# A one-core attention, expert and feed-forward kernel: the first pair's queries loaded and prepared ahead of its keys, and the early weights loaded into rooms that are free

## The chip, the cores and the metric

One core of a Trainium2 chip runs the whole program in one launch. The metric is the device time in microseconds (us), the median of its runs; the profile is of one execution.

## What is computed

Three layers, one after another, in float32 at the interfaces:

```python
# linear attention: B=4, H=8, S=576, D=64
q_s = softmax(q, axis=-1)                  # over each query's 64 elements
k_s = softmax(k, axis=2)                   # over the 576 positions
kv  = einsum('bhsd,bhse->bhde', k_s, v)
x   = einsum('bhsd,bhde->bhse', q_s, kv)   # to x of 2304 tokens x 512
# experts: 8 of them, 512 -> 1024 -> 512
P = exp(x @ w_gate - max); 8 rounds of row and column normalising
out = sum_e P[:, e] * (relu(x @ w1[e]) @ w2[e])
# feed-forward: 512 -> 2048 -> 512, weights in float64
h = out @ w_in;  g = h * clip(h + 3, 0, 6) / 6;  y = g @ w_out
```

## The kernel before

**Numbers.** A float32 matrix product is made of three products of 16-bit halves (high by high, high by low, low by high). An operand is therefore scaled by a power of two taken from its largest magnitude, and split: ScalarE (ACT) writes the high half, VectorE (DVE) the low half (`split`, L216 and L217, for weights; L669 and L670 for tokens). The up-projection of a 512-wide weight slice uses Strassen's scheme: seven products of two-by-two blocks instead of eight, so tokens and weights are each kept in seven *forms* (QB11 and so on of the tokens, QA11 and so on of the weights, L34 and L35).

**Tiling.** The 2304 tokens are 18 tiles of 128; three tiles make a group, two groups a pair: PAIRS = [(0, 1), (3, 4), (2, 5)]. Weights come in slices of 512 columns: 16 slices of the experts (`s` 0 to 15), then four of the feed-forward layer. A step (s, p) runs slice s on pair p: two bursts of up-products (`up_burst`, matmuls of L957), and between them the down-products of the step before (`down_tile`, L1057). Step (0, 0) is the first, (1, 0) the second. Pairs 1 and 2 of the tokens are made while these run.

**Before step (0, 0) there is a prologue**, whose order is written out by hand (L1112 to 1196, `tc.manual_schedule()`): on every engine, and in the queue of SP that issues the DMAs, its instructions come in that order. From there to a later step the Tile scheduler sets the order, and it may place instructions of later steps among the prologue's. Two batches (`t0`) come first. The prologue before:

- SP issues the keys (`load_k`, 8 DMAs into part of `xbuf`), two thirds of the queries, which are groups 0 and 1 (`load_q`, 8 DMAs into `qbuf`, tiles 9 to 14 of `acc`), the values (8 DMAs into `v_room`, tiles 0 to 8 of `acc`), the first slice of `w1` (into `raw`) and the gate's weights.
- DVE takes the keys' maximum over positions (`kmax`, L481 to 484) chunk by chunk as they land; PE turns it and spreads it back (`ktr`, `kback`), DVE subtracts it (`ksub`, L519), ACT takes exponentials (`kexp`).
- DVE takes both groups' query maxima (L583), subtracts them (L590), ACT takes exponentials (L594). POOL copies the values next to a column of ones (`vcopy`, L469); PE multiplies keys by values (`kv`, L541).
- For each group DVE sums the exponentials and takes the reciprocal (`qsum`, L598 to 600); POOL scales the queries in four pieces (`qn`, L606), PE turns each piece (`qtr`, L615), ACT copies it out (L623). `turned(g)` is that chain of four pieces.
- DVE takes the first `w1` slice's maximum (`a1_scale`, L246 to 254; across partitions by a small matmul, L193, and a reduction, L195), POOL its three first sums (`a1_sums`, L282). SP issues the first `w2` slice (`a2`) into `w2_room`, tiles 9 to 12 of `acc`, part of `qbuf`. DVE normalises the products of keys and values (`kvout`), takes their maximum (L560), from which `kvkeep` makes their scale.
- The seven token forms (`forms`: f[0] QB11, f[1] QT1, f[2] QB21, f[3] QB22, f[4] QT2, f[5] QT3, f[6] QT4) alternate with the seven splits of `w1` (a1[0] QA11, a1[1] QS1, a1[2] QA12, and so on), then come the maximum and splits of `w2` (`a2`). A form is 16 matmuls (`xset`, L635), four more for some (`onto`, L676), two copies of ACT and two subtractions of DVE. f[3] to f[6] are built up in one bank, QB22's. `bank` gives QB22 the banks A and B, the others C and D or the two of `ps_d`.
- SP issues the second slice of `w1` (`w1_1`, into `raw` again), and the second two batches' keys and values.

In step (0, 0), a burst's products go into the banks X (A or D), Y (B) and Z (C); the first product is X (form 0), then Y (QT1 by QS1), then Z (QB21 by QA12). The steps of `w1_1` after its load (maximum, sums on POOL, seven splits) and those of the second two batches are put on a queue (`ticks`) and one to three of them are issued after each product. After step (0, 0), SP issues the second two batches' queries and the second `w2` slice (`w2_1`, into `raw`), whose maximum and splits follow in the queue behind ten steps of the keys and queries.

Of the kernel before, what the change touches and what calls it, by code (L numbers as in the profile page):

```python
# [36 lines left out]
TOP1 = 12  # L37
# [6 lines left out]
def tile_attention_moe_ffn(  # L44
# [218 lines left out]
    def fill(s):  # L263

        return [None] * (5 if s in (2, 3) else 3)

    def w1_steps(s, first=False):

        st = {}
        dst = w1op[s % 2]  # L270
# [24 lines left out]
        steps = [load] + fill(s) + w_scale(f"a{s}_", st, s, TOP1)  # L295
# [123 lines left out]
    def attention(pr):  # L419
# [19 lines left out]

        def load_rows(dst, r0, n):  # L440
            for i in range(2):
                for c in range(NKC):
                    nc.sync.dma_start(
                        out=dst[:, 2 * c + i], in_=rows(q, i)[:, c].rearrange("n (r d) -> n r d", d=D)[:, r0 : r0 + n]
                    )
# [10 lines left out]
        def load_v(room=None):  # L456
            if room is not None:
                for c in range(NKC):
                    load(room, v, slice(c, c + 1))
                return  # L460
            for c in range(NKC):
                for i in range(2):
                    nc.sync.dma_start(
                        out=vt[:, 2 * c + i, :, :D], in_=rows(v, i)[:, c].rearrange("n (r d) -> n r d", d=D)
                    )
# [254 lines left out]
        t.update(vcopy=vcopy, v_ones=v_ones, load_k=load_k, load_v=load_v, load_q=load_q, load_qlast=load_qlast, kmax=kmax, ktr=ktr, mT=mT,  # L720
# [217 lines left out]
    def up_burst(s, p, qf, hs, between):  # L938
# [57 lines left out]
        if not ffn:  # L996
# [3 lines left out]
            prod("Y", 4, True, False)  # L1000
            prod("Z", 1, True, True)
# [111 lines left out]
    with tc.manual_schedule():  # L1113
# [9 lines left out]
        w2_room = half(acc[:, NJ // 2 : NJ // 2 + NFC, :])  # L1123
# [3 lines left out]
        t0["load_k"]()  # L1127
        t0["load_q"]()
        t0["load_v"](v_room)
        a1_load()  # L1130
        nc.sync.dma_start(out=wg, in_=w_gate.rearrange("(c p) e -> p c e", p=P))
        t0["v_ones"]()
# [11 lines left out]
        def keys(c):  # L1144
            t0["ksub"]((c,))
            t0["kexp"](c)

        run([K("kmax", (0,)), lambda: turn(0), K("kmax", (1,)), lambda: turn(1), lambda: back_(0), K("kmax", (2, 3)),
             lambda: turn(2), lambda: turn(3), lambda: back_(1), lambda: keys(0), lambda: back_(2),
             lambda: keys(1), lambda: back_(3), lambda: keys(2), lambda: keys(3)])  # L1150

        ga, gb = PAIRS[0]
        run([K("qmax", ga), K("qmax", gb), K("qsub", ga), K("qexp", ga), K("qsub", gb), K("qexp", gb)])
        run([K("vcopy", c, v_room) for c in range(NKC)])
        run([K("kv_", c) for c in range(NKC)])
        t0["qsum"](ga)

        def turned(g):
            for c in range(NKC + 1):
                if c > 0:  # L1160
                    t0["qtr"](c - 1, g, t0["qn", c - 1])
                if c < NKC:
                    t0["qn_"](c, g)
                    t0["qn", c] = t0["qn"]

        turned(ga)
        t0["qsum"](gb)
        turned(gb)
        run(a1_scale[:3])
        run(a1_sums)  # L1170
        a2.pop(0)()
# [3 lines left out]
        run(t0["max"][1:])  # L1175

        count = [0]

        def bank(name, qd, i):
            if qd == QB22:  # L1180
                return ps_u.tile([P, 512], F32, tag="AB"[i], name=name)[:, :GN]
            count[0] += 1
            if (count[0] - 1) % 4 < 2:
                return ps_u.tile([P, 512], F32, tag="CD"[i], name=name)[:, :GN]
            return ps_d.tile([P, DM], F32, tag="d", name=name)[:, :GN]

        f = t0["forms"](0, bank)
        run([f[0], a1[0], f[1], a1[1], f[2], a1[2], f[3], a1[3], f[4], a1[4]] + a2[:6] + [f[5], a1[5]] + a2[6:8]
            + [f[6], a1[6]] + a2[8:])
        w1_1 = w1_steps(1)  # L1190
        w1_1[0]()
# [77 lines left out]
    w2_1 = w2_steps(1)  # L1269
    w2_1[0]()  # L1270
# [72 lines left out]
```

## Time and profile before

| | |
|---|---|
| median of three runs | 1872.18 us (1871.99 to 1873.56) |
| the profiled execution's own time | 1873.7 us |
| span from its first to its last instruction | 1871.9 us |
| granted TensorE clock, mean | 0.997 of full |
| PE (TensorE matmul) busy | 1828.0 us, 98% |
| DVE / ACT / POOL busy | 1173.4 / 863.9 / 610.2 us |

Times in the views are microseconds from the span's start. A timeline row gives start, duration, engine, line, operation, what it writes and reads, the count of like instructions run together and, in brackets, how long the engine sat idle before it and what ended that. `PEld` is the weight load, `SPq` an issue of a DMA by SP.

### The profile page before, as it was taken

The numbers are of one execution on the slowest core, as the hardware profiler recorded it, in microseconds if no ns is written. First come the engines' busy times: TensorE is split into PE (matmuls) and PEld (weight loads), VectorE is DVE, ScalarE is ACT, GpSimd is POOL, SyncE is SP. The second block draws the span as 40 slices with busy tenths as digits, with TensorE's granted clock in tenths as the row PEclk, the third lists the DMA queues.
The fourth block names the chain that finished last, engine by engine and source line by source line (L and its number), as shares of the span: only waits on it lengthen the run. The fifth ranks groups of instructions, "written<-read, shape, count | busy, mean of one in ns | idle before, by whom it ended". The sixth has DMA issues, their size and how long they took to land.

```text
span 1871.9 us, 26846 instructions
## 1 busy us (share of the span) xinstructions
PE 1828.0 (98%) x10596; PEld 967.5 (52%) x10596; DVE 1173.4 (63%) x2086; ACT 863.9 (46%) x1651; POOL 610.2 (33%) x581
## 2 busy tenths in 40 slices
PE   5899999999999999999999999999999999999999
PEld 3455555555555555555555555555555555555554
DVE  7982866555565656565656556565636697678554
ACT  4656454444444434343444434444434466545432
POOL 3323344333333333324342424233323233313121
PEclk9999999999999999999999999999999999999999
DMA  6600011111111020201111102011100100010001
GB/s 219 172 6 1 24 46 34 45 52 62 36 61 57 23 74 23 74 23 57 40 57 40 66 32 75 22 62 35 62 29 1 45 1 23 23 46 23 1 29 73
DMA packets 50926, 87.72 MB, mean 47 GB/s; under 512 B 12656, under 2 KB 16752, under 8 KB 50800
## 3 DMA queue, kind: packets, MB, share of 16 engines
q1 hardware_dynamic: 50800, 86.01, 13.9%
q8 instruction: 83, 1.36, 0.3%
q14 instruction: 43, 0.35, 0.1%
HBM read 72.89 MB, written 13.11 MB: 46 GB/s over the span
## 4 chain that ended last, share of the span: by engine, by line
PE 85%; DVE 9%; ACT 3%; issue 1%; POOL 1%; DMA 0%; SPq 0%; DVEq 0%; POOLq 0%; ACTq 0%
PE y L1057 44%; PE X L957 19%; PE Y L957 9%; PE Z L957 5%; PE B L957 2%; PE C L957 2%; PE A L957 2%; DVE w1buf L217 2%; DVE r L965 1%; DVE g L982 1%; PE D L957 1%; DVE scr L395 1%; DVE acc L1067 1%; DVE xbuf L391 1%; ACT h L983 0%
## 5 line engine op out<-in xcount | busy, mean ns | idle before, releaser
L1057 PE MATMUL y<-w2buf,h 128*128 128x512 f16 x4320 | 992.7, 379 | 3.0 <-POOL h L989 2.8
L957 PEld LDWEIGHTS <-w1buf 128*128 128x128 f16 x5040 | 490.9, 98 | 369.4 <-issue 17.6
L1057 PEld LDWEIGHTS <-h 128*128 128x128 f16 x4320 | 421.3, 98 | 471.5 <-POOL h L989 3.2
L989 POOL TENSOR_TENSOR h<-r,h 128x384 f16<-128x384 f32 x288 | 273.6, 951 | 850.4 <-ACT h L988 794.1
L957 PE MATMUL X<-xbuf,w1buf 128*128 128x384 f16 x2304 | 439.7, 327 | 3.1 <-ACT r L970 2.5
L970 ACT ACTIVATE r<-X 128x384 f32<-128x384 f32 x384 | 187.1, 488 | 518.6 <-PE X L957 509.3
L1067 DVE SCALAR_TENSOR_TENSOR acc<-y,cf,acc 128x512 f32<-128x512 f32 x252 | 188.3, 747 | 223.4 <-PE y L1057 223.1
L957 PE MATMUL Y<-xbuf,w1buf 128*128 128x384 f16 x1152 | 220.3, 327 | 2.5 <-DVE xbuf L391 2.0
L965 DVE SCALAR_TENSOR_TENSOR r<-Y,r 128x384 f32<-128x384 f32 x192 | 106.1, 553 | 79.7 <-PE Y L957 41.8
L988 ACT CAST h<-r 128x384 f16<-128x384 f32 x288 | 147.0, 510 | 8.2
L984 POOL TENSOR_TENSOR h<-g,h 128x384 f16<-128x384 f32 x72 | 67.2, 934 | 252.1 <-ACT h L983 207.7
L987 ACT ACTIVATE r<-r 128x384 f32<-128x384 f32 x192 | 99.9, 520 | 99.2 <-DVE r L965 98.2
L957 PE MATMUL Z<-xbuf,w1buf 128*128 128x384 f16 x576 | 110.5, 326 | 2.2 <-ACT w1buf L216 1.2
L965 DVE SCALAR_TENSOR_TENSOR r<-Z,r 128x384 f32<-128x384 f32 x96 | 53.1, 553 | 87.6 <-PE Z L957 85.2
L983 ACT CAST h<-g 128x384 f16<-128x384 f32 x96 | 48.9, 511 | 95.5 <-DVE g L982 95.4
L991 ACT ACTIVATE h<-r 128x384 f16<-128x384 f32 x96 | 50.1, 522 | 89.0 <-DVE r L965 89.0
L992 DVE SCALAR_TENSOR_TENSOR h<-r,h 128x384 f16<-128x384 f32 x96 | 57.5, 599 | 51.4 <-ACT h L991 51.2
L981 ACT ACTIVATE g<-r,three,zi 128x384 f32<-128x384 f32 x96 | 67.3, 703 | 3.9 <-DVE r L965 3.0
L982 DVE SCALAR_TENSOR_TENSOR g<-g,r 128x384 f32<-128x384 f32 x96 | 60.8, 637 | 11.6 <-ACT g L981 9.3
L965 DVE SCALAR_TENSOR_TENSOR r<-B,r 128x384 f32<-128x384 f32 x48 | 26.6, 554 | 51.1 <-PE B L957 47.4
L957 PE MATMUL C<-xbuf,w1buf 128*128 128x384 f16 x288 | 54.6, 326 | 1.6 <-DVE r L965 1.6
L957 PE MATMUL B<-xbuf,w1buf 128*128 128x384 f16 x288 | 54.6, 326 | 0.9 <-DVE r L965 0.6
(620 smaller groups left out, 1569.1 us busy)
## 6 DMA issues: line engine op xcount, KB each, us to landing
raw<-in_moe_w_dram SPq DMA_DIRECT2D x31, 1024.0 KB, 5.7
scr<-in_moe_w_in_dram SPq DMA_DIRECT2D x16, 512.0 KB, 4.2
scr<-in_moe_w_out_dram SPq DMA_DIRECT2D x16, 512.0 KB, 3.5
out_dram<-acc SPq DMA_DIRECT2D x18, 256.0 KB, 2.0
win<-scr SPq DMA_DIRECT2D x16, 256.0 KB, 3.3
wout<-scr SPq DMA_DIRECT2D x16, 256.0 KB, 2.2
raw<-win SPq DMA_DIRECT2D x4, 1024.0 KB, 5.0
raw<-wout SPq DMA_DIRECT2D x4, 1024.0 KB, 5.6
```

What stands on the lines that cost most here:

```text
L957: nc.tensor.matmul(bank[b], w[:, i, wi, c, fs], x[:, i, xi, c, :], start=(first and n == 0), stop=(last and n == 5), skip_group_check=True,)
L965: nc.vector.scalar_tensor_tensor(out=o, in0=bank[b], scalar=sign * H_DOWN, in1=i1, op0=ALU.mult, op1=ALU.add)
L970: nc.scalar.activation(o, bank[b], fn, scale=H_DOWN)
L981: nc.scalar.activation(r, c, AF.Relu, scale=zi, bias=three)
L982: nc.vector.scalar_tensor_tensor(out=r, in0=r, scalar=6.0 * KAPPA, in1=c, op0=ALU.min, op1=ALU.mult)
L984: eng.tensor_sub(h[:, 1, :], r, h[:, 0, :])
L987: nc.scalar.activation(c, c, AF.Relu)
L988: nc.scalar.copy(h[:, 0, :], c)
L989: eng.tensor_sub(h[:, 1, :], c, h[:, 0, :])
L992: nc.vector.scalar_tensor_tensor(out=h[:, 1, :], in0=c, scalar=0.0, in1=h[:, 0, :], op0=ALU.max, op1=ALU.subtract)
L1057: nc.tensor.matmul(ps, hs[grp][fc][:, hi, ts_], w[:, wi, fc, :], start=(n == 0), stop=(n == 11))
L1067: nc.vector.scalar_tensor_tensor(out=acc[:, j, :], in0=ps, scalar=cf, in1=acc[:, j, :], op0=ALU.mult, op1=ALU.add)
```

## The change

The prologue is reordered:

- The first group's queries (ga) are loaded ahead of the keys, in two DMAs with runs of 768 bytes, the second group's (gb) behind them, in two more; keys and values come in four DMAs each.
- ga's maximum, subtraction and exponentials precede the keys' work; ga's sums and turning follow it. gb's maximum and subtraction come after these, its sums behind a1[0], and its turning between f[0] and f[1].
- The first `w2` slice goes to tiles 0 to 3 of `acc`, part of the values' room, and is issued behind `vcopy`. The second `w1` slice is issued in the prologue's first row of loads, into the buffer `w2buf[1]`. The second `w2` slice goes to `raw`, ahead of the second two batches' keys.
- The forms' order is f[0], f[2], f[1], f[3] and so on; QB21 has the banks A and B, QB11 and QT1 have C and D, QB22 those of `ps_d`. In both bursts of step (0, 0), Z comes before Y.

```diff
--- before.py
+++ after.py
@@ -264,9 +264,10 @@
 
         return [None] * (5 if s in (2, 3) else 3)
 
-    def w1_steps(s, first=False):
+    def w1_steps(s, first=False, flat=raw):
 
         st = {}
+        rw = view(flat, 0, [P, NKC, FS])
         dst = w1op[s % 2]
         Fh = FS // 2
         A = {(i, j): rw[:, 2 * j : 2 * j + 2, i * Fh : (i + 1) * Fh] for i in range(2) for j in range(2)}
@@ -292,7 +293,7 @@
                 lambda: (tt(A[0, 1], A[0, 1], S2, "tensor_sub")(), sp(QS2, S2)()),
                 sp(QS3, A[1, 0]), sp(QA22, A[1, 1]), sp(QS4, A[0, 1]),
             ]
-        steps = [load] + fill(s) + w_scale(f"a{s}_", st, s, TOP1)
+        steps = [load] + fill(s) + w_scale(f"a{s}_", st, s, TOP1, flat)
         steps[-1] = (lambda f=steps[-1]: (f(), res[s].__setitem__("s1", st["s"])))
         steps += [
             tt(S1, A[1, 0], A[1, 1], "tensor_add"), sp(QA11, A[0, 0]),
@@ -437,6 +438,23 @@
             for u in range(n):
                 load(kt, k, slice(u * NKC // n, (u + 1) * NKC // n))
 
+        def chunk(src, c):
+
+            return src[b0 : b0 + 2].rearrange("b h s d -> b (h s d)").rearrange(
+                "b (c n x) -> n b c x", n=P, x=QR * D)[:, :, c]
+
+        def load_chunk(dst, src, c):
+            nc.sync.dma_start(out=dst.rearrange("p (c i) r d -> p c i (r d)", i=2)[:, c], in_=chunk(src, c))
+
+        def load_group(g):
+
+            r0 = gl(g) * GJ * D
+            for i in range(2):
+                nc.sync.dma_start(
+                    out=qbuf.rearrange("p (c i) r d -> p c i (r d)", i=2)[:, :, i, r0 : r0 + GJ * D],
+                    in_=rows(q, i)[:, :, r0 : r0 + GJ * D],
+                )
+
         def load_rows(dst, r0, n):
             for i in range(2):
                 for c in range(NKC):
@@ -456,7 +474,7 @@
         def load_v(room=None):
             if room is not None:
                 for c in range(NKC):
-                    load(room, v, slice(c, c + 1))
+                    load_chunk(room, v, c)
                 return
             for c in range(NKC):
                 for i in range(2):
@@ -717,7 +735,7 @@
 
         a, gap, b = across_max(lambda: t["am"], f"kv{pr}", st)
         t["max"] = [lambda: (kvmax(), a()), gap, b, kvkeep]
-        t.update(vcopy=vcopy, v_ones=v_ones, load_k=load_k, load_v=load_v, load_q=load_q, load_qlast=load_qlast, kmax=kmax, ktr=ktr, mT=mT,
+        t.update(load_chunk=lambda c: load_chunk(kt, k, c), load_group=load_group, vcopy=vcopy, v_ones=v_ones, load_k=load_k, load_v=load_v, load_q=load_q, load_qlast=load_qlast, kmax=kmax, ktr=ktr, mT=mT,
                  kback=kback, ksub=ksub, kexp=kexp, kv_=kv, kvout=kvout, qmax=qmax, qsub=qsub, qexp=qexp, qsum=qsum,
                  qn_=qn, qtr=qtr, forms=forms, items=items)
         return t
@@ -997,8 +1015,9 @@
             r1, r2, r3, r4 = (rt(f"r{n}_{nm}") for n in range(1, 5))
             prod("X", 0, True, False)
             copy(r1, "X")
-            prod("Y", 4, True, False)
-            prod("Z", 1, True, True)
+
+            for b, i, last in ((("Z", 1, True), ("Y", 4, False)) if s + p == 0 else (("Y", 4, False), ("Z", 1, True))):
+                prod(b, i, True, last)
             prod("X", 5, False, False)
             add(r1, "Z", r1)
             copy(r2, "X")
@@ -1120,15 +1139,22 @@
 
         t0, t1 = attention(0), attention(1)
         K = call(t0)
-        w2_room = half(acc[:, NJ // 2 : NJ // 2 + NFC, :])
+
+
+        w2_room = half(acc[:, :NFC, :])
         v_room = view(half(acc[:, : NJ // 2, :]), 0, [P, H, QR, D])
         a1_load, a1_scale, a1_sums, a1 = w1_steps(0, first=True)
         a2 = w2_steps(0, w2_room)
-        t0["load_k"]()
-        t0["load_q"]()
+        w1_1 = w1_steps(1, flat=w2buf[1])
+        ga, gb = PAIRS[0]
+        t0["load_group"](ga)
+        for c in range(NKC):
+            t0["load_chunk"](c)
+        t0["load_group"](gb)
         t0["load_v"](v_room)
         a1_load()
         nc.sync.dma_start(out=wg, in_=w_gate.rearrange("(c p) e -> p c e", p=P))
+        w1_1[0]()
         t0["v_ones"]()
 
         held = {}
@@ -1145,50 +1171,47 @@
             t0["ksub"]((c,))
             t0["kexp"](c)
 
+        run([K("qmax", ga), K("qsub", ga), K("qexp", ga)])
         run([K("kmax", (0,)), lambda: turn(0), K("kmax", (1,)), lambda: turn(1), lambda: back_(0), K("kmax", (2, 3)),
              lambda: turn(2), lambda: turn(3), lambda: back_(1), lambda: keys(0), lambda: back_(2),
              lambda: keys(1), lambda: back_(3), lambda: keys(2), lambda: keys(3)])
-
-        ga, gb = PAIRS[0]
-        run([K("qmax", ga), K("qmax", gb), K("qsub", ga), K("qexp", ga), K("qsub", gb), K("qexp", gb)])
         run([K("vcopy", c, v_room) for c in range(NKC)])
+        a2.pop(0)()
         run([K("kv_", c) for c in range(NKC)])
-        t0["qsum"](ga)
-
-        def turned(g):
-            for c in range(NKC + 1):
-                if c > 0:
+
+        def turned(g, c0=0, c1=NKC):
+            for c in range(c0, c1 + 1):
+                if c > c0:
                     t0["qtr"](c - 1, g, t0["qn", c - 1])
-                if c < NKC:
+                if c < c1:
                     t0["qn_"](c, g)
                     t0["qn", c] = t0["qn"]
 
+        t0["qsum"](ga)
         turned(ga)
-        t0["qsum"](gb)
-        turned(gb)
+        run(a1_sums[:2])
+        run([K("qmax", gb), K("qsub", gb), K("qexp", gb)])
         run(a1_scale[:3])
-        run(a1_sums)
-        a2.pop(0)()
+        run(a1_sums[2:])
         t0["kvout"]()
         run(t0["max"][:1])
         run(a1_scale[3:])
         run(t0["max"][1:])
-
-        count = [0]
+        a1[0]()
+        t0["qsum"](gb)
+
 
         def bank(name, qd, i):
             if qd == QB22:
-                return ps_u.tile([P, 512], F32, tag="AB"[i], name=name)[:, :GN]
-            count[0] += 1
-            if (count[0] - 1) % 4 < 2:
-                return ps_u.tile([P, 512], F32, tag="CD"[i], name=name)[:, :GN]
-            return ps_d.tile([P, DM], F32, tag="d", name=name)[:, :GN]
+                return ps_d.tile([P, DM], F32, tag="d", name=name)[:, :GN]
+            return ps_u.tile([P, 512], F32, tag=("AB" if qd == QB21 else "CD")[i], name=name)[:, :GN]
 
         f = t0["forms"](0, bank)
-        run([f[0], a1[0], f[1], a1[1], f[2], a1[2], f[3], a1[3], f[4], a1[4]] + a2[:6] + [f[5], a1[5]] + a2[6:8]
-            + [f[6], a1[6]] + a2[8:])
-        w1_1 = w1_steps(1)
-        w1_1[0]()
+        run([f[0], lambda: turned(gb, 0, 2), f[2], lambda: turned(gb, 2), a1[2], f[1], a1[1], f[3], f[4], a1[3]]
+            + a2[:4] + [f[5], a1[4]] + a2[4:6] + [f[6], a1[5]] + a2[6:8] + [a1[6]] + a2[8:])
+
+        w2_1 = w2_steps(1)
+        w2_1[0]()
         t1["load_k"](2)
         t1["load_v"]()
         done.add(("w1", 0))
@@ -1266,8 +1289,6 @@
     prev = step(0, 0, None)
     need(("w1", 1))
     t1["load_q"]()
-    w2_1 = w2_steps(1)
-    w2_1[0]()
     t1["rooms"] = R[8:] + R[:8]
     one = beside(t1)
     put(ticks, one[:10])
```

## Rows read from the trace of the kernel before

**Rows 1.** The page: its span, and busy time and share of each engine.
```profile
span 1871.9 us, 26846 instructions
...
PE 1828.0 (98%) x10596; PEld 967.5 (52%) x10596; DVE 1173.4 (63%) x2086; ACT 863.9 (46%) x1651; POOL 610.2 (33%) x581
```

**Rows 2.** Busy by stretch: PE, PEld, DVE, ACT, POOL (x); clock, DMA share, GB/s.
```profile
10.00:15.00 5.00, 1.83 (x10) 0.76 (x10) 4.33 (x7) 0.07 (x1) 0.00 (x0) 1.00 1.07 382
...
25.00:30.00 5.00, 1.71 (x70) 1.33 (x61) 4.86 (x7) 2.50 (x3) 1.89 (x3) 1.00 0.62 166
...
75.00:80.00 5.00, 5.00 (x30) 2.71 (x29) 3.11 (x5) 3.26 (x7) 3.44 (x3) 1.00 1.14 302
```

**Rows 3.** Timeline of DVE, 0 to 75 us: start, us, what, [idle before <-releaser].
```profile
4.40 0.69 DVE L481 TENSOR_TENSOR scr<-xbuf 128x512 f32<-128x512 f32 x1 [3.39 <-DMA xbuf<-in_k_dram]
...
10.56 1.22 DVE L481 TENSOR_TENSOR scr<-xbuf 128x1024 f32<-128x1024 f32 x1 [0.98 <-DMA xbuf<-in_k_dram]
...
19.00 3.41 DVE L583 TENSOR_REDUCE qm<-acc 128x24 f32<-128x1536 f32 x2
...
22.32 3.42 DVE L590 TENSOR_TENSOR acc<-acc,qm 128x1536 f32<-128x1536 f32 x2
...
27.87 1.70 DVE L598 TENSOR_REDUCE qm<-acc 128x24 f32<-128x1536 f32 x1
...
30.04 2.28 DVE L246 TENSOR_REDUCE am_a__416<-raw 128x1 f32<-128x1024 f32 x2
...
35.29 0.29 DVE L195 TENSOR_REDUCE m_a__436<-cm_a__434 128x1 f32<-128x128 f32 x1 [0.89 <-PE cm_a__434 L193]
...
39.73 1.02 DVE L670 TENSOR_TENSOR xbuf<-f,xbuf 128x384 f16<-128x384 f32 x2 [1.33 <-ACT xbuf L669]
...
46.95 1.01 DVE L670 TENSOR_TENSOR xbuf<-f,xbuf 128x384 f16<-128x384 f32 x2
...
56.71 2.74 DVE L217 SCALAR_TENSOR_TENSOR w2buf<-acc,ws_b__570,w2buf 128x512 f16<-128x512 f32 x4
...
72.79 2.28 DVE L481 TENSOR_TENSOR scr<-xbuf 128x2048 f32<-128x2048 f32 x1
```

**Rows 4.** Timeline of PE, 0 to 102 us.
```profile
28.99 0.55 PE L615 MATMUL qT<-ident,qn 128*128 128x128 f32 x3 [3.04 <-POOL qn L606]
...
37.63 2.84 PE L635 MATMUL f<-qt,xbuf 64*64 64x192 f32 x32 [1.77 <-ACT xbuf L567]
...
41.43 1.53 PE L635 MATMUL f<-qt,xbuf 64*64 64x192 f32 x32
...
54.73 1.15 PE L957 MATMUL Y<-xbuf,w1buf 128*128 128x384 f16 x6
...
67.11 0.61 PE L1057 MATMUL y<-w2buf,h 128*128 128x512 f16 x2 [2.81 <-POOL h L989]
...
101.38 0.23 PE L193 MATMUL cm_b__892<-identb,wm_b__878 128*128 128x128 bf16 x1 [1.05 <-DVE wm_b__878 L254]
```

**Rows 5.** Timeline of POOL, 0 to 70 us.
```profile
28.11 6.36 POOL L606 TENSOR_TENSOR qn<-acc,qm 128x384 f32<-128x384 f32 x8 [6.24 <-DVE qm L600]
...
61.02 1.28 POOL L282 TENSOR_TENSOR wtmp<-raw 128x512 f32<-128x512 f32 x1
```

**Rows 6.** Timeline of SP's DMA issues.
```profile
21.89 8.25 SPq L443 DMA_DIRECT2D acc<-in_q_dram  x14
...
55.51 0.38 SPq L276 DMA_DIRECT2D raw<-in_moe_w_dram  x1
...
77.87 0.38 SPq L312 DMA_DIRECT2D raw<-in_moe_w_dram  x1
```

**Rows 7.** Timeline of ACT, 39 to 41 us.
```profile
39.22 0.86 ACT L669 CAST xbuf<-f 128x384 f16<-128x384 f32 x2 [1.64 <-PE f L635]
...
39.96 0.73 ACT L216 ACTIVATE w1buf<-raw,ws_a__438 128x512 f16<-128x512 f32 x1
```

**Rows 8.** Instructions on the tile wgm: duration min/median/max ns, first and last start us.
```profile
L798 DVE TENSOR_REDUCE wgm<-wg x1: 175/175/175, 111.7 to 111.7; 128x1 f32<-128x32 f32 x1
```

## The prediction

> **What bounds the kernel now.** I read the page first: PE is busy for 98% of the span [rows 1]. PE is the bound of the long middle and end, which the change does not touch. So only time that PE loses at the start can be won, and it is lost for good: a matmul that starts later ends later.
>
> Next I read the timelines of the first 100 us, engine by engine. Until about 60 us it is not PE that sets the pace but DVE. Its first wait is for keys until 4.40; the last keys are taken at 10.56 after a wait of 0.98; from 19.00 it works almost without a break through the queries, the first weights' maximum and the products of keys and values, waits 0.89 before 35.29 and 1.33 before 39.73, then makes the low halves of forms and weights until 59.45 (56.71 and 2.74) [rows 3]. So I follow DVE's order, and ask at each step what it waits for after the change.
>
> **The load order.** The first group's queries are 128 x 8 x 192 floats, 0.79 MB, in runs of 768 bytes, and now stand before the keys. While the kernel before loads such runs (25 to 30 us) the DMA engines move 166 GB/s at a busy share of 0.62, or 268 GB/s at full share; long runs reach 382 at 1.07, or 357 [rows 2]. So the keys come 2.9 or 2.2 us later, and I take 2.9, the rate of the same run length: the last keys at 13.5 instead of 10.56. In that time DVE does the first group's maximum and subtraction, half of 3.41 and of 3.42 [rows 3], 3.4 us that used to come after the keys. **Gain 0.5 us** (0.5 to 1.2). The queries themselves should land near 5.5, later than the first keys' 4.40, as 0.79 MB stand against the 0.59 MB of the first key chunk.
> The Trainium skill, DMA: Bandwidth & Descriptors, section Specifications, holds 512 bytes for enough to reach line rate. By that rule the keys would come only 2.2 us later and the sum below would be 0.7 lower, an estimate; the 268 GB/s of the 768-byte stretch agree with it only in part, since issue gaps lie in it too.
>
> The number of loads in the first row falls by 12 issues of SP; the DMA engines are full there (share 1.07 [rows 2]), so this is worth nothing. The second `w1` slice queues behind the gate's weights and the first `w2` slice behind `vcopy`; neither is used before 45 us, so their landing is covered. The second `w2` slice now waits in SP's queue until `raw` is free, with the second keys and values behind it; before, the second `w1` slice held them at the same place, 55.51 [rows 6], and the keys are first used at 72.79 [rows 3]. A shift of 2 us is covered by 17 us less the transfer: nothing.
>
> **Up to the first form.** Summing the second group's exponentials takes from 27.87 to 30.04, 2.2 us [rows 3], and leaves the path to the key-value scale. The wait of 0.89 before 35.29 is for a small matmul behind the second group's transposes on PE; these are moved behind, so it goes. DVE's work before that wait ended at 34.40 (35.29 less 0.89); now at 34.4 - 0.5 - 2.2 = 31.7. From there to the first form's matmuls took 37.63 - 34.40 = 3.2 [rows 3, 4], now 2.3: **34.0 instead of 37.63**.
>
> **From the first form on, most of this is given back.** The second group stands in between. DVE's order is now a1[0], the sums, f[0]. The key scale's copy on ACT ends at 34.0, a1[0] takes 0.73 on ACT [rows 7] and 0.7 on DVE (a quarter of 2.74 [rows 3]), to 35.4; the sums to 37.6; f[0]'s low halves (1.0) to 38.6, against 40.75 before. Then DVE has nothing: f[2] stands in PE's queue behind two pieces of the second group. POOL takes 0.8 for each piece (6.36 for eight [rows 5]), so 39.2; the transposes 0.55 and a hand-over of 0.1 [rows 4], 39.9; f[2]'s 16 matmuls 0.8 to 1.4 (half of 1.53 or of 2.84 [rows 4]), I take 1.1, 41.0; ACT's copy 0.43 (half of 0.86 [rows 7]), 41.5. **A new wait of 2.9 us**, longer than the 0.89 and 1.33 that go. The next, a1[2], stands on ACT behind f[2]'s other half and two copies of turned pieces: 1.1 us more. f[4] is added to the bank that f[3]'s subtraction must have read, and a1[3], which used to fill that gap, now comes after: 0.5. Added up with 1.0 for each form and 0.7 for each split, DVE has f[0] to f[4] and four splits done at 49.6; before, it had the same at 47.96 [rows 3]. **Loss 1.7 us**, 0.2 with the short ends (f[2] at 0.8, the keys at 2.2, no gap at f[4]), 3.9 if f[2] takes 1.4 and two forms stand behind an up-product of about 1 us in PE's queue. The last `w2` split goes from 59.45 to about 61.
>
> **What PE gets back.** Three things, all in the steps that follow.
> - Bank B. The first Y product ran at 54.73 [rows 4], since QB22 held bank B up to f[6]. Now QB21 has it and is done by 42.5, so Y runs some 8 us earlier, and one product fewer is left when the last split is made: **1.0** (0 to 1.15, the row).
> - POOL. PE waits 2.81 before 67.11 for POOL's `h` [rows 4], which stands behind the second `w1` slice's sums, from 61.02, 1.28 each [rows 5]; that slice was issued only at 55.51 [rows 6]. Now it is there before 30, and the sums fit where POOL is free. But the products after that wait need the slice's splits, which DVE must still make and which are now late by 1.7. I take about half, **1.5** (0 to 2.8).
> - The second `w2` slice was issued at 77.87 [rows 6]; its maximum kept PE waiting 1.05 before 101.38 [rows 4]. It can now be taken earlier: DVE has time, being busy 3.11 of 5 us from 75 to 80 [rows 2]. **1.05** (0 to 2.28, the price of a maximum [rows 3]).
>
> Sum: 1.7 - 1.0 - 1.5 - 1.05 = -1.85. The profiled execution took 1873.7, 1.8 beyond its span of 1871.9, and becomes 1871.9; the median of the runs is 1.5 below that execution, so 1872.18 becomes **1870.3**. The bounds together reach from -6.0 to +3.9.
>
> **The rivals.** About 0.2%, 3.74 us, is what a measurement of this kernel can tell from no change: 1868.4 and 1875.9.
> - *Faster: the new wait is filled.* The Tile scheduler may place later steps among the prologue's; 14 loads of a later step stand at 21.89 [rows 6]. If it puts the second `w1` slice's maximum, 2.28, into the 2.9 us, that slice is ready earlier by as much, the 2.81 wait goes whole, and so does 2.3 at the second `w2` slice: 1.7 - 2.3 - 2.8 - 2.3 - 1.15 = -6.85, **1865.3**. Against it: the gate's maximum, a small one on weights loaded in the first row, ran only at 111.7 [rows 8], so maxima have not been brought far forward. 0.35.
> - *Slower: the second group's chain decides.* POOL, PE and ACT hand over four times between f[0] and f[1], and the up-products that may now start go into PE's queue ahead of forms. The long end of 3.9 holds, nothing is won back: **1876.1**. This decides if f[2]'s subtraction starts after 42.5. For it speaks that these engines are in order; against it that DVE, not PE, held the forms before. 0.12.
> - *Level: the credits do not come*, because DVE is full until about 100 us and a wait of PE that goes only comes back elsewhere: +1.7, **1873.9**. 0.17.
>
> The forecast has 0.36. Faster by over 0.2%: most of the first rival (0.30) and the low side of the forecast (0.07), 0.37; slower 0.12; the rest, 0.51, within. The range reaches to the first rival's time and a little below, and up to the slower one's: 1864.8 to 1876.0.
>
> **What would show it.** The first maximum of queries near 5.5 and the last keys at 13.5; f[0]'s matmuls at 34; an idle stretch of DVE of some 3 us between f[0]'s and f[2]'s subtractions; the first Y near 46; the second `w1` slice's sums on POOL before 60, and no wait for `h` near 65; the second `w2` slice's maximum before 90. If that idle stretch is missing because a maximum fills it, the first rival holds. If the order of steps beyond (1, 0), which the scheduler also sets, shifts by several us by itself, all of this is wrong.

## The result, and the profile after

The changed kernel takes **1885.66 us** (median of 4 runs, 1885.41 to 1886.82), the kernel before 1872.55 beside it: ratio **1.0069**, 95% interval 1.0054 to 1.0084. It is slower by 13 us, outside the range of the prediction. The page of the profiled execution:

```profile
span 1884.1 us, 26832 instructions
...
PE 1830.7 (97%) x10596; PEld 968.1 (51%) x10596; DVE 1173.4 (62%) x2086; ACT 864.0 (46%) x1651; POOL 614.1 (33%) x581
```

The busy times are those of [rows 1] but for 2.7 us of PE; the span is 12.2 us longer. So PE stands idle or slow for longer, and the first question is where. The timeline of PE answers it, read later than the prediction had read it. The kernel before:

```profile
107.60 1.15 PE L957 MATMUL Y<-xbuf,w1buf 128*128 128x384 f16 x6
...
135.31 1.89 PE L1057 MATMUL y<-w2buf,h 128*128 128x512 f16 x8
137.04 1.14 PE L957 MATMUL X<-xbuf,w1buf 128*128 128x384 f16 x6
```

The kernel after:

```profile
119.28 1.14 PE L975 MATMUL Y<-xbuf,w1buf 128*128 128x384 f16 x6
...
138.35 0.49 PE L694 MATMUL f<-xbuf,minus 128*128 128x384 f16 x2
138.67 10.52 PE L1076 MATMUL y<-w2buf,h 128*128 128x512 f16 x48
149.03 1.14 PE L975 MATMUL X<-xbuf,w1buf 128*128 128x384 f16 x6
```

The last row of each fence is the first product of step (0, 1), **the start of the second pair**: 137.04 before, 149.03 after. From there to the end of the span both take the same, 1871.9 - 137.0 = 1734.9 and 1884.1 - 149.0 = 1735.1 us. The whole loss lies ahead of this row. The same 1150 matmuls of PE stand ahead of it in both kernels: before, PE is busy with them for 106.2 us and idle for 30.8; after, for 109.0 and 40.0. So 9.2 of the 12.0 us are more idle time of PE, 4.1 of them between 70 and 97 us and 3.9 behind, and 2.8 are slower matmuls.

Two things must be done for the second pair to start: PE must have built its last form (the rows f, which go on as DVE and ACT read the forms out), and PE must have done the down-products of step (1, 0), the rows y, 72 in number. DVE's last row of the forms ends 1.1 us after the last f in every kernel below. Before, the last up-product of step (1, 0), the first row of the fence, runs at 107.60, and all but 8 of the 72 y behind it are done in the gaps that the second pair's own chain leaves on PE; after, it runs at 119.28, there are 84 y behind it (some of step (0, 0) among them), and 48 are left when the last form is built, 10.52 us of nothing else. PE is behind with its work by then, and the last up-product is 11.7 us late: the gaps come, and the y are not ready to fill them.

Why the products are late is seen on DVE, whose rows answer to [rows 3]:

```profile
5.39 1.75 DVE L601 TENSOR_REDUCE qm<-acc 128x24 f32<-128x1536 f32 x1 [4.39 <-DMA acc<-in_q_dram]
...
12.68 1.23 DVE L499 TENSOR_TENSOR scr<-xbuf 128x1024 f32<-128x1024 f32 x1
...
33.27 0.29 DVE L195 TENSOR_REDUCE m_a__390<-cm_a__388 128x1 f32<-128x128 f32 x1 [1.16 <-PE cm_a__388 L193]
...
39.08 0.95 DVE L688 TENSOR_TENSOR xbuf<-f,xbuf 128x384 f16<-128x384 f32 x2
43.91 1.02 DVE L688 TENSOR_TENSOR xbuf<-f,xbuf 128x384 f16<-128x384 f32 x2 [3.87 <-ACT xbuf L687]
45.67 0.75 DVE L217 SCALAR_TENSOR_TENSOR w1buf<-raw,ws_a__392,w1buf 128x512 f16<-128x512 f32 x1 [0.74 <-ACT w1buf L216]
...
49.24 1.73 DVE L601 TENSOR_REDUCE qm<-acc 128x24 f32<-128x1536 f32 x1
...
56.34 1.20 DVE L246 TENSOR_REDUCE am_a__601<-w2buf 128x1 f32<-128x1024 f32 x1
...
60.28 1.21 DVE L246 TENSOR_REDUCE am_a__601<-w2buf 128x1 f32<-128x1024 f32 x1
...
64.41 1.75 DVE L608 TENSOR_TENSOR acc<-acc,qm 128x1536 f32<-128x1536 f32 x1
66.08 4.05 DVE L217 SCALAR_TENSOR_TENSOR w2buf<-acc,ws_b__559,w2buf 128x512 f16<-128x512 f32 x4
```

Three things stand between the first form (39.08) and the first `w2` splits (66.08): the wait of 3.87 for the second group, the second `w1` slice's maximum (1.20 and 1.21), and work on the second batches' queries (1.73 and 1.75). The splits end at 70.1; [rows 3] had 59.45. POOL, SP and PE, in that order, one fence each:

```profile
48.47 1.27 POOL L283 TENSOR_TENSOR wtmp<-w2buf 128x512 f32<-128x512 f32 x1 [0.63 <-DVE w1buf L217]
```

```profile
22.20 22.86 SPq L461 DMA_DIRECT2D acc<-in_q_dram  x22
60.32 0.38 SPq L313 DMA_DIRECT2D raw<-in_moe_w_dram  x1
```

```profile
35.60 0.88 PE L653 MATMUL f<-qt,xbuf 64*64 64x192 f32 x16 [1.73 <-ACT xbuf L585]
40.19 1.69 PE L633 MATMUL qT<-ident,qn 128*128 128x128 f32 x6 [3.70 <-POOL qn L624]
...
50.37 1.14 PE L975 MATMUL Y<-xbuf,w1buf 128*128 128x384 f16 x6
```

SP issues 22 loads of queries in one row where [rows 6] had 14. The last eight, from 40.16, are the second batches' first two groups (`load_q`; q_held below moves these eight, and the 14 stay). The kernel before issues two of these eight early and six late, behind the second keys and values:

```profile
34.49 0.80 SPq L443 DMA_DIRECT2D acc<-in_q_dram  x2
...
74.31 3.46 SPq L443 DMA_DIRECT2D acc<-in_q_dram  x6
```

Six of the eight write into the tiles of `qbuf` in which the first `w2` slice lay until its splits ended at 59.45; the other two do not. The change gives that slice the values' room, so nothing holds the six any more. DVE's first work on these queries comes at 49.24 instead of 90.15 us.

### The profile page after: what moved, and what is told of

Same layout as the page of the kernel before. It is cut to its first block, busy times and chain, and to the rows that moved or that the text cites. A ratio compares the mean times of both kernels' runs of the same rounds, so it can differ in the third digit from the quotient of the medians.

```text
span 1884.1 us, 26832 instructions
## 1 busy us (share of the span) xinstructions
PE 1830.7 (97%) x10596; PEld 968.1 (51%) x10596; DVE 1173.4 (62%) x2086; ACT 864.0 (46%) x1651; POOL 614.1 (33%) x581
## 4 chain that ended last, share of the span: by engine, by line
PE 84%; DVE 11%; ACT 3%; issue 2%; POOL 0%; DMA 0%; SPq 0%; DVEq 0%; ACTq 0%
PE y L1076 44%; PE X L975 19%; PE Y L975 9%; PE Z L975 5%; DVE w1buf L217 2%; PE B L975 2%; PE C L975 2%; PE A L975 2%; DVE r L983 1%; DVE g L1000 1%; PE D L975 1%; DVE w2buf L217 1%; DVE acc L1086 1%; DVE scr L396 1%; DVE xbuf L392 1%
## 5 line engine op out<-in xcount | busy, mean ns | idle before, releaser
L1000 DVE SCALAR_TENSOR_TENSOR g<-g,r 128x384 f32<-128x384 f32 x96 | 60.9, 637 | 11.7 <-ACT g L999 9.4
```

The costliest lines, as they stand in the source:

```text
L1000: nc.vector.scalar_tensor_tensor(out=r, in0=r, scalar=6.0 * KAPPA, in1=c, op0=ALU.min, op1=ALU.mult)
```

## The experiments

Each kernel below computes the reference in full. The table gives, from each profiled execution, the start of the last up-product of step (1, 0), the end of the second pair's forms on DVE, the y that are left behind the last f, the start of the second pair, and the span less that start, and the ratio of the timed runs.

```
kernel                last Y   forms  y left   start  span-start  ratio [95%]
before                107.60   136.6     8    137.04    1734.9
after                 119.28   140.0    48    149.03    1735.1    1.0069 [1.0054, 1.0084]
q_held                109.09   137.2    31    142.60    1734.9    1.0040 [1.0027, 1.0053]
late_w                107.99   135.9    31    141.32    1735.0    1.0033 [1.0020, 1.0046]
both_held             108.31   139.9    27    144.44    1734.9    1.0037 [1.0024, 1.0050]
q_early               108.81   136.3    16    138.51    1735.5    1.0025 [1.0014, 1.0036]
p1_load_order         106.94   135.9     8    136.37    1734.9    0.9997 [0.9988, 1.0007]
p2_forms              115.80   144.7     8    145.15    1734.9    1.0048 [1.0033, 1.0063]
p3_weights            120.19   130.9    63    143.23    1734.9    1.0038 [1.0023, 1.0053]
p4_weights_q_held     117.43   136.4    44    144.65    1734.9    1.0039 [1.0025, 1.0053]
g1_chain_ahead        113.27   142.2     8    142.62    1734.8    1.0034 [1.0021, 1.0048]
g2_chain_behind       110.99   140.8     8    141.23    1734.9    1.0021 [1.0011, 1.0030]
g3_weights_all_held   102.86   132.0    36    138.46    1734.8    1.0024 [1.0015, 1.0033]
g4_repaired           103.28   134.0    27    138.59    1734.9    1.0021 [1.0012, 1.0031]
z_first               105.72   134.6     8    135.08    1734.8    0.9996 [0.9986, 1.0005]
h1_repaired_rate      100.36   136.7     0    135.41    1735.0    0.9991 [0.9981, 1.0000]
h3_before_rate        102.01   139.1     0    137.80    1734.9    1.0001 [0.9992, 1.0011]
r1_after_rate         105.03   143.1     0    141.87    1734.9    1.0038 [1.0025, 1.0052]
r2_order_and_z        106.19   135.2     8    135.63    1735.0    0.9999 [0.9990, 1.0008]
r3_repaired_again      99.81   136.3     0    135.01    1735.0    0.9994 [0.9985, 1.0003]
```

In 19 of the 20 the span less the start is 1734.8 to 1735.1 (q_early: 1735.5): this one row carries the time. All 20 have 1150 matmuls of PE ahead of it. A late last up-product is not the only way to have y left: g3 and g4 have it earlier than before and leave 36 and 27. Where no y are left, the start comes right behind the last f, and so 1.3 us ahead of DVE's end. One profile is one execution; the runs of before spread over some 3 us, so a start is good to 1 or 2 us.

**First, parts of the change undone.**

q_held: the second batches' query loads behind their values, so that they land late again.

```diff
         t1["load_v"]()
+        t1["load_q"]()
...
-    t1["load_q"]()
```

> The changed kernel, with the second two batches' query loads written behind the second values in the hand-made order; nothing else differs. Theory A (the early landing of these queries let the scheduler put their maxima and subtractions, 1.75 us each, into DVE's row before the w2 splits and the second w1 splits): these four move behind, and 5 to 8 of the 13 us go: 1877.5 to 1880.5. Rival B (the loss is the wait between f[0] and f[2], 3.87 us, and what follows from the second group's chain): 1883 to 1886. Rival C (the second w1 slice's maximum and sums brought forward): 1883 to 1886 as well.

q_early: the kernel before with these loads ahead of the second `w1` slice.

```diff
+        t1["load_q"]()
         w1_1[0]()
```

> The kernel before, with the second two batches' query loads moved ahead of the second w1 slice's load; nothing else differs. Theory A: their maxima and subtractions come ahead of the second w1 slice's splits on DVE, 3.5 to 7 us later start of step (1, 0): 1875.5 to 1879. Rivals B and C: no change, 1871 to 1874.

late_w: the change with the second weights loaded into `raw` as before.

```diff
-        w1_1 = w1_steps(1, flat=w2buf[1])
...
-        w2_1 = w2_steps(1)
-        w2_1[0]()
+        w1_1 = w1_steps(1)
+        w1_1[0]()
...
     t1["load_q"]()
+    w2_1 = w2_steps(1)
+    w2_1[0]()
```

> The changed kernel, with the second w1 slice loaded into raw behind the forms and the second w2 slice behind step (0, 0), as before; the second queries still land early. Theory A: 1882 to 1887, little changed. Rival C (the early second weights did it): 1874 to 1878. Rival B: 1883 to 1886.

both_held: q_held, and the second `w1` slice's maximum put by hand behind the first `w2` splits.

```diff
+        run(w1_1[4:7])
...
-    put(ticks, w1_1[4:])
+    put(ticks, w1_1[7:])
```

> As q_held, and the second w1 slice's maximum written behind the first w2 splits. Theory A: what is left after q_held is the 2.4 us of that maximum in front of the w2 splits and the 2 to 4 us of the wait between f[0] and f[2]: 1875 to 1878. Rival B: 1882 to 1886. Rival C: 1873 to 1877.

Measured: 1879.55, 1876.73, 1879.54 and 1879.58, against 1872.66 before. Holding the queries gives back 6.1 of the 13 us, so that part is real; but each undoing gives back only about half, holding both gives no more than holding one, and late_w and both_held came out in none of the ranges that I had written. No single piece is the cause. q_early is not early queries alone: its eight loads wait for the first `w2` slice's tiles, and they push the second `w1` slice back from 55.51 to 61.55. Its 1.0025 is the price of both.

```profile
56.76 4.69 SPq L443 DMA_DIRECT2D acc<-in_q_dram  x8
61.55 0.38 SPq L276 DMA_DIRECT2D raw<-in_moe_w_dram  x1
```

late_w shows that the tiles held these loads in the kernel before, and not the second `w1` slice, which waits for `raw` in front of them: in late_w that slice waits as before (59.02), but the first `w2` slice lies in the values' room, and all 22 loads go in one row.

```profile
22.09 22.35 SPq L461 DMA_DIRECT2D acc<-in_q_dram  x22
```

**Second, each part alone, on the kernel before.** p1_load_order takes only the new order of loads, with the first group's queries worked on first; p2_forms only the second group behind the first form, the order and banks of the forms, and Z ahead of Y; p3_weights only the early weights and their rooms.

```diff
-        w1_1 = w1_steps(1)
+        w1_1 = w1_steps(1, flat=w2buf[1])
...
+        w1_1[0]()
         t0["v_ones"]()
```

p4_weights_q_held is p3_weights with the query loads of q_held. p2_forms, and g2_chain_behind below, also issue the first `w2` slice some 7 us later (40.66 and 40.96 instead of 33.70), since its tiles are those of the second group's queries; DVE does not wait for it.

> The kernel before, with only the load order of the change: first group's queries ahead of the keys and worked first, second group's behind, keys and values in four DMAs each; everything after is ordered as before. Theory A (the time goes where work of the second two batches and second weights enters DVE's row): none of that enters here, so -1 to +1: 1871.5 to 1873.5. Rival B (the hand-made order costs it): the load order has a share of 2 to 4 us: 1874.5 to 1877.

> The kernel before, with only the second half of the change's order: second group's sums behind a1[0], its turning between f[0] and f[1], the forms' new order and banks, Z ahead of Y in step (0, 0); loads as before. Theory A: at most the 1.7 us that the prediction counted as loss, less the 1.0 for bank B: 1872 to 1874.5. Rival B: the wait of 3.9 us between f[0] and f[2] comes through whole, with the one behind it: 1875.5 to 1878.

> The kernel before, with only the early weights: first w2 slice in the values' room, second w1 slice in w2buf[1] in the first row of loads, second w2 slice ahead of the second keys. The second queries' loads then come early by themselves, and their maximum and subtraction stand ahead of the w2 splits on DVE, as does the second w1 slice's maximum. Theory A: most of the 13 us, 1878 to 1883. Rival B: 1870 to 1873.

> As p3_weights, with the second queries' loads written behind the second values. Theory A: 5 to 7 us less than p3_weights, what is left being the second w1 slice's maximum (2.4 us) ahead of the w2 splits: 1873 to 1876. Rival B: 1870 to 1873, as p3_weights.

Measured: 1873.05 (1873.26 before: nothing), 1881.86, 1880.04 and 1880.86. The forms cost 8.6 us alone and the weights 6.8; the changed kernel, with both and the load order, loses 13.1, not their sum. Holding the queries, worth 6.1 us in the changed kernel, gives nothing on the weights alone, against what I expected of p4. The two parts fail in two ways, which the table shows. In p2_forms DVE is late: the forms end 8 us later and the second pair starts behind 8 y, as before. Its DVE timeline has the wait:

```profile
42.84 1.02 DVE L670 TENSOR_TENSOR xbuf<-f,xbuf 128x384 f16<-128x384 f32 x2 [3.88 <-ACT xbuf L669]
```

In p3_weights DVE is early, the forms end at 130.9, and PE is late: 63 y are left. Its DVE timeline, then its PE timeline:

```profile
53.63 1.21 DVE L246 TENSOR_REDUCE am_a__613<-w2buf 128x1 f32<-128x1024 f32 x1
...
62.26 1.75 DVE L591 TENSOR_TENSOR acc<-acc,qm 128x1536 f32<-128x1536 f32 x1
63.93 4.05 DVE L217 SCALAR_TENSOR_TENSOR w2buf<-acc,ws_b__571,w2buf 128x512 f16<-128x512 f32 x4
```

```profile
129.64 13.76 PE L1058 MATMUL y<-w2buf,h 128*128 128x512 f16 x63
143.23 1.14 PE L958 MATMUL X<-xbuf,w1buf 128*128 128x384 f16 x6
```

What is worked on early there is the second slice's and the second pair's; the first `w2` splits, for which step (0, 0)'s down-products wait, come behind it.

**Third, p2_forms and the weights taken apart.** g1_chain_ahead leaves the second group ahead of the forms; g2_chain_behind moves only the second group.

```diff
         turned(ga)
+        t0["qsum"](gb)
+        turned(gb)
...
-        run([f[0], lambda: turned(gb, 0, 2), f[2], lambda: turned(gb, 2), a2.pop(0), a1[2], f[1], a1[1], f[3], f[4], a1[3]]
+        run([f[0], f[2], a1[2], f[1], a1[1], f[3], f[4], a1[3]]
```

g3_weights_all_held is p4_weights_q_held with the maximum held as in both_held. g4_repaired is the changed kernel with all three suspects undone: second group ahead, queries held, maximum held.

> The kernel before with the new order of the forms, their new banks and Z ahead of Y, but the second group's sums and transposes left ahead of the forms, as before. Theory 'chain': what the forms' part of the change costs (8 us) is the wait of DVE for the second group between the first and the second form; without it the last w2 split ends by 60.5 (59.45 before, 63.4 with the chain behind), and the time is 1871 to 1874.5. Rival 'order': the new order, the banks or Z first cost it; then the time is 1878 or more although DVE has no wait of over 1.5 us there.

> The kernel before with only the second group's sums and transposes moved behind the first form; order of the forms, banks and Y ahead of Z as before. Theory 'chain': DVE waits 3 to 5 us between the first and the second form, the last w2 split ends at 62 to 65, and the time is 1877 to 1883. Rival 'order': the time stays within 1870.5 to 1875.

> The kernel before with only the early weights, the second queries' loads held behind the second values, and the second w1 slice's maximum put behind the first w2 splits by hand. Theory 'brought forward': the early weights cost 7 us since DVE and PE take the second slice's maximum (2.4 us) and the second queries' work between the first forms and splits; with both held DVE's work up to the last w2 split is that of before (59 to 60.5) and the time is 1871 to 1875. Rival 'what follows': with the second slice on hand POOL's sums and its splits run among step (0,0)'s products all the same and delay h, and the order of the steps behind it changes; then the time stays at 1878 to 1881.

> The changed kernel with its three suspects undone: the second group's sums and transposes ahead of the forms, the second queries' loads behind the second values, the second w1 slice's maximum behind the first w2 splits. If the wait for the chain and the work brought forward are the causes and add up: 1870 to 1875, and what is left is order of loads, banks, form order and early weights. If the order of the steps behind (0,0) costs by itself: 1877 or more.

Measured: 1879.23, 1877.02, 1876.98 and 1877.04 (1872.45 before). g3 lies outside both of its ranges. My theory for g1 fell: its last `w2` split ends at 60.2, as expected, and it is still 6.8 us slower. The PE timeline of g1_chain_ahead shows by what:

```profile
61.70 1.14 PE L957 MATMUL X<-xbuf,w1buf 128*128 128x384 f16 x6
67.08 0.61 PE L1057 MATMUL y<-w2buf,h 128*128 128x512 f16 x1 [4.25 <-POOL h L989]
67.48 0.31 PE L193 MATMUL cm_a__624<-identb,wm_a__615 128*128 128x128 bf16 x1
```

and that of the kernel before at the same place:

```profile
63.38 0.22 PE L193 MATMUL cm_a__624<-identb,wm_a__615 128*128 128x128 bf16 x1
...
63.92 0.38 PE L1057 MATMUL y<-w2buf,h 128*128 128x512 f16 x1
```

`cm_a` is the small matmul of the second `w1` slice's maximum. Before, it stands ahead of the y that waits for POOL's `h` (2.81, [rows 4]); in g1 it stands behind it, so DVE's splits of that slice wait with PE. It runs 67.48 - 63.38 = 4.1 us later: 1.0 because the maximum itself ends later (DVE waits 1.25 for the slice to land), and 3.1 for its place behind the y, of which DVE is idle for 2.88. The forms end 5.6 later. Nothing in g1's edit names this matmul, and no run moves it alone: that its place makes the 5.6 is read from the traces. g2 has it ahead of the y and shows that the moved group costs by itself too, 4.6 us, with a wait of 5.9 on DVE between the first two forms and the last `w2` split 3.4 later.

Against p4, g3 prices the second slice's maximum ahead of the first `w2` splits at 3.9 us on the weights alone; in the changed kernel both_held shows nothing for it beyond q_held. g3 and g4 have their forms 3 to 5 us sooner than before and still start later, with 36 and 27 y left. In g4 PE had been busy for 3.5 us more than in the kernel before between 40 and 90 us (46.42 and 42.90; these windows do not show the 6.7 of an expectation below), and lost this and more, on DVE and then on PE:

```profile
87.84 3.42 DVE L601 TENSOR_REDUCE qm<-acc 128x24 f32<-128x1536 f32 x2 [0.16 <-issue]
91.17 4.14 DVE L608 TENSOR_TENSOR acc<-acc,qm 128x1536 f32<-128x1536 f32 x2
95.23 3.39 DVE L217 SCALAR_TENSOR_TENSOR w2buf<-raw,ws_b__884,w2buf 128x512 f16<-128x512 f32 x4
98.55 3.40 DVE L616 TENSOR_REDUCE qm<-acc 128x24 f32<-128x1536 f32 x2
...
102.72 0.50 DVE L983 SCALAR_TENSOR_TENSOR r<-Y,r 128x384 f32<-128x384 f32 x1
```

```profile
103.28 2.08 PE L975 MATMUL Y<-xbuf,w1buf 128*128 128x384 f16 x6 [4.88 <-DVE r L983]
```

The addition `r`, half a microsecond long, empties a bank that PE wants; it stands behind 14 us of other work, on the second batches' queries and the second `w2` slice.

**Fourth, that order mended.** h1_repaired_rate is g4_repaired with the second pair's steps put out one per product instead of two, and the rest among the down-products. h3_before_rate has this alone on the kernel before, r1_after_rate alone on the changed kernel; z_first has only Z ahead of Y.

```diff
-    rate[0] = 2
+    rate[0] = 1
     prev = step(1, 0, prev)
+    rate[0] = 4
     for grp in range(2):
```

> The kernel before with only product Z ahead of Y in step (0,0). It splits the loss of g1_chain_ahead (first up-product of the second pair at 142.6 us of the span, 137.0 before): if putting Z first makes it, by another order of POOL's and PE's work about 65 us, this run has 1876 to 1880 and POOL's h keeps PE and the second w1 slice's small matmul waiting 4 us or more; if the order and banks of the forms make it, 1871 to 1874 with a wait near the 2.81 of before.

> g4_repaired with step (1,0)'s side work put out at one step per product instead of two, and four per half down-tile behind it, so that the additions r of (1,0) stand ahead of the second queries' sums in DVE's queue. In g4_repaired PE was 6.7 us ahead of before at 90 us and lost all of it at 98 to 103 in a wait of 4.9 for such an addition. Theory 'the second pair's start sets the time': span is 1734.9 plus the time of the second pair's first up-product; without that wait the product starts at 134.5 to 137, and the time is 1870 to 1873.5, at or below before. Rival 'DVE is full': the forms then come later by what DVE does first, the product stays at 138 or more, and the time at 1875 or more.

> The kernel before with the same rates of side work in step (1,0) as h1_repaired_rate. Theory: before, the second pair's forms on DVE end at 136.6 and its first up-product follows at 137.0, so DVE's chain sets the start, and nothing is gained by the rates: 1871.5 to 1877. Rival 'the rates alone are better': 1870 or less.

> The changed kernel with only the rates of side work in step (1,0) of h1_repaired_rate; its chain behind the first form, its early second queries and its second w1 maximum in the prologue's row stay. If the late chain and the work brought forward cost by themselves, the second pair still starts at 144 us or more and the time is 1879 or more; if PE's order behind (1,0) was the whole loss, it falls to 1874 or less.

Measured: 1872.76, 1871.57 and 1873.17 (1873.25 before), and 1879.36 (1873.15 before). In h1_repaired_rate `r` comes ahead of the sums, PE's wait there falls to 1.05, and no y is left. Its DVE timeline, then its PE timeline:

```profile
99.76 0.55 DVE L983 SCALAR_TENSOR_TENSOR r<-Y,r 128x384 f32<-128x384 f32 x1
100.23 1.74 DVE L616 TENSOR_REDUCE qm<-acc 128x24 f32<-128x1536 f32 x1
```

```profile
135.08 0.49 PE L694 MATMUL f<-xbuf,minus 128*128 128x384 f16 x2
135.41 1.14 PE L975 MATMUL X<-xbuf,w1buf 128*128 128x384 f16 x6
```

That is some 14 us less than the changed kernel. The rates alone give nothing to the kernel before, whose forms then end at 139.1, and take the changed kernel from 1.0069 to 1.0038: half of its loss goes with the order in step (1, 0), the other half stays, with no y left and forms that end at 143.1, 3.1 us later than at the old rate. Z ahead of Y costs nothing alone, so what g1 lost came with the order and banks of the forms, unless Z first costs only beside them.

Last, whether anything of the change is worth keeping: r2_order_and_z puts p1_load_order and z_first together, r3_repaired_again repeats h1_repaired_rate with five rounds.

> The kernel before with the two parts of the change that cost nothing alone: the load order with the first group's queries first (p1_load_order) and Z ahead of Y in step (0,0) (z_first). If the second pair's start adds them up (0.6 and 1.9 sooner in their profiled runs), it starts near 134.5 and the time is 1869 to 1871.5; if they were the scatter of single profiles, 1871.5 to 1874.

> h1_repaired_rate again, with more rounds, since the end of its interval was at 1.0000. By its first-product time of 135.4 us, 1.6 sooner than before: a ratio of 0.9985 to 0.9995. If that was the scatter of one call: 0.9995 to 1.001.

Measured: 1872.62 and 1871.80 (1873.15 before), 0.9999 [0.9990, 1.0008] and 0.9994 [0.9985, 1.0003]. The repaired kernel came out 1.7 and 1.35 us faster in its two timings, less than a measurement can tell from no change. No version here beats the kernel before beyond doubt.

## Why the prediction was wrong

**What held.** The load order was worth nothing that can be measured (0.5 forecast; p1_load_order 0.9997). The first maximum of queries came at 5.39 (near 5.5 forecast), the last keys at 12.68 instead of 10.56 (they land at 12.5 instead of 10.4), so 2.1 later: nearer to 2.2, the rate of long runs, than to the 2.9 that I took. The Trainium skill, DMA: Bandwidth & Descriptors, section Specifications, holds 512 bytes for enough to reach line rate; this trace agrees with it, with 2.1 us for 0.79 MB in runs of 768 bytes. The idle stretch on DVE was there, 3.87 (2.9 forecast), then 0.74 (1.1). The sums on POOL came before 60 (48.47), and the wait for `h` near 65 was gone. The first form's matmuls came at 35.60, not 34.0, since the wait of DVE that I had struck out stayed: 1.16 before 33.27.

**The first step that failed: where I stopped reading.** "Only time that PE loses at the start can be won, and it is lost for good" is true, but I followed the first 100 us and added up waits of PE that would go. What counts is the start of the second pair at 137, the later of two things, the forms and PE's y. A wait that goes from PE at 65 is worth nothing if the forms set the start, and DVE's lead is worth nothing if y are left. What the three credits stood for came about, the first by half (no wait for `h` near 65, the second `w2` slice's maximum at 89.8 instead of 97.27, Y at 50.37 instead of 54.73, where I had it near 46), and bought nothing: p3_weights, made for the second and third of them, costs 6.8 us where I had 1.5 and 1.05 as gains. Other waits came in their place, as my level rival had it, which I gave 0.17: PE waits 0.85 before 71.24, 2.07 before 78.13 and 0.69 before 79.90 in the changed kernel, none of them in the kernel before.

**The second: "maxima have not been brought far forward".** I read it from one small maximum [rows 8]. After the change the second slice's maximum stands at 56.34 and 60.28, ahead of the first `w2` splits, with the second pair's query work. My rival "the new wait is filled" had the mechanism half right: the maximum did come forward, but behind the idle stretch of 3.87 and not into it, and there it costs 3.9 us on the weights alone (p4 against g3).

**The third: loads "worth nothing".** I counted what the change issues sooner and left out what it stops holding back: six of the second batches' query loads had been held by the first `w2` slice, which lay in their tiles. q_held prices this at 6.1 us in the changed kernel; beside the weights alone, p4 shows nothing for it.

**The term that was mis-sized** is the loss from the first form on: 1.7, with a long end of 3.9. In p2_forms the last `w2` split ends 4.0 later, the long end, and the start of the second pair 8.1 later, since `cm_a` then stands behind the y that waits for `h`. The terms that I gave there add up to 49.2, not 49.6, so the loss was 1.2 by my own figures; p2_forms has the same five forms and four splits done at 51.0, 3.1 later than before. The condition of my slower rival, the second subtraction after 42.5, was met (43.91), and its mechanism is right; its price was half of what p2_forms shows.

**The closing caution** came true in kind: the order of the automatic part shifted by several us, in step (1, 0) itself rather than beyond it. What stays open is why the scheduler put `cm_a` behind that y in g1_chain_ahead, as order and banks of the forms were not tried apart, and how much each of the three pieces costs beside the others, as their prices do not add up: h1_repaired_rate, which undoes them and mends the order in step (1, 0), shows only that together they are the loss.

## What to carry to other kernels

Find the row from which two traces run in step (here the second pair's first product; span less its time was the same to 0.7 us in every kernel), and count an early gain only if it moves the later of the things which that row waits for. Data that arrive early are no gain by themselves where a scheduler orders the queues: it puts work that has become ready ahead of work that others wait for, and a half-microsecond addition or a small matmul behind it cost 3 to 5 us here. Before moving a buffer, list what else its old place held back.

## What the hardware showed that I had not expected

PE's clock fell after the new gaps, and this made them dearer. Windows of the kernel after (us, then busy time of PE, PEld, DVE, ACT, POOL, the granted clock, DMA share, GB/s):

```profile
56.00:58.00 2.00, 0.83 (x5) 0.31 (x4) 2.00 (x5) 1.80 (x4) 0.38 (x1) 1.00 0.00 0
58.00:60.00 2.00, 1.01 (x6) 0.32 (x5) 2.00 (x5) 0.00 (x0) 0.89 (x1) 1.00 0.00 0
60.00:62.00 2.00, 1.04 (x5) 0.47 (x4) 2.00 (x7) 0.87 (x2) 0.00 (x0) 0.57 0.12 25
62.00:64.00 2.00, 2.00 (x9) 0.96 (x8) 0.66 (x5) 1.96 (x4) 0.00 (x0) 0.50 0.89 333
64.00:66.00 2.00, 2.00 (x8) 0.92 (x7) 1.87 (x3) 2.00 (x5) 0.50 (x1) 0.50 1.02 357
66.00:68.00 2.00, 1.96 (x9) 0.78 (x7) 2.00 (x3) 2.00 (x3) 2.00 (x2) 0.72 1.03 384
```

PE was busy for about half of 56 to 62 us, and then ran at 0.50, the lower of its two levels, while it was fully busy: six X products took 2.08 us there instead of 1.14. The shares missing from 60 to 68 add up to 2 x (0.43 + 0.50 + 0.50 + 0.28) = 3.4 us; a second such stretch, from 124 to 130, has 1.7. From 60 us on the kernel before has one, behind its wait for `h` (0.58 and 0.57 in 68 to 72, 1.7 us). Part of this falls on time in which PE is idle anyway: for the same 1150 matmuls ahead of the second pair PE is busy 2.8 us longer, so about 2.8 of the 12 us are clock, paid for waits.
